# A fused convolution and SwiGLU kernel: the sixth block pair put in the Strassen form, with a new hand-written order of all engines

## The chip, the cores and the metric

The kernel runs on one core of a Trainium2 chip. The metric is the device time of one execution in microseconds (us). Five engines work side by side: TensorE (PE, matrix products; PEld is its weight load), VectorE (DVE), ScalarE (ACT), GpSimd (POOL) and SyncE (SP, which here only issues DMAs). Each engine runs its own instructions strictly in the order in which they were recorded, and waits at an instruction until the semaphores that it names have been reached.

## The reference, cut to what matters

```python
# x: (8, 4096, 192), weight: (8 heads, 7 taps)
w = softmax(weight, axis=-1)
y[b, s, h, g] = sum_k w[h, k] * x_pad[b, s + k, h, g]       # causal, 7 taps, 24 channels a head
y = y.reshape(32768, 192)
xn = y / sqrt(mean(y * y, axis=-1) + 1e-6) * rms_g
g = xn @ w_gate                                             # 192 -> 1536
v = xn @ w_val                                              # 192 -> 1536
out = (g * sigmoid(g) * v) @ w_out                          # 1536 -> 192, float32
```

## The kernel before

**Tiling.** The 32768 tokens are worked on in 32 "pairs" of 1024 tokens (two groups of 512), numbered 0 to 31. Pairs 0 and 1 take plain fp32 products while the weights are made ready; pairs 2 to 31 take the form that this text is about. The 1536 hidden columns are cut into 12 blocks of 128, and these into six block pairs j = 0 to 5. For each j and for the two token groups there are four results ("cells") a, b, c, d, each with a gate half and a value half in PSUM. The contraction over 192 rows runs in three slices of 64 rows, written as a 2x2 block scheme. Each fp32 operand is split into three fp32r parts, so one product of two blocks is three passes, each once for the gate half of the array and once for the value half: one word of LINE, such as `P6.4`, is six matmul instructions (recorded at L899).

**Two forms of a block pair.** `FORM[j]` says which. Form 0 (plain) takes 12 products, `Aa` to `Ed`. Form 1 (Strassen) takes 11, named P1 to P7 and Q1 to Q4, and pays for it with elementwise work: `f1` copies cell a into cell b's bank once P1 is in it, `f3` copies cell c into SBUF once P5 is in it, `f4` writes c = b + that copy after P6 and before P7, and `f5` writes d = b + that copy after P7 and before Q3, P4 and Q4. Before, j = 0, 2, 4 have form 1.

**After the products.** `g` (ACT) takes Silu of a cell's gate half, `m` (DVE) multiplies it with the value half into `ht` and so frees the PSUM bank pair. There are four bank pairs; each cell holds one from its first product to its `m`. The products with w_out are in a Strassen form too: 42 steps `oN.j` of eight narrow matmuls each (L923), fed by sums `h1` to `h4` of the four cells (L950). At the end X, Y, Z are brought together (`c1`, `s7`, `c2`, `C22`, `C21`, `T..`) and stored (`st`).

**The input side, for the next pairs.** `ld` loads x (8 DMAs of one head each), `cv0` to `cv6` are the convolution taps (`cv0` on ACT, the others on DVE), `sq`, `red`, `pow`, `bc`, `mul` normalise, `pl` writes the result to a scratch in DRAM (8 DMAs), `ft` reads it back transposed (6 DMAs). `x1` to `x4` make the Strassen sums of the operands, and `n`, `l`, `d` split operand group 0 to 4 into its three parts.

**What sets the order.** Everything is in three hand-written lists of words. A word is engine letter (V DVE, G POOL, A ACT, S SP), name and block; a trailing `-` means the pair before, `+` the next pair, `++` the one after that; `pN` issues the next N words of LINE on PE. FIRST is the window in which pair 1 is computed and the weights of pairs 2 to 31 are made (each `W` is one step of `prepare`); ORDER is one steady window and is run for w = 2 to 32. Within an engine the words are the order of execution. LINE is the order of PE's products and steps.

**The ring.** The split weights (`wd`, in DRAM) come through ten slots of 192 KB. When the last product that needs a slot has been issued, `ring_load` puts the load of the next piece in SP's queue at that place. `R` (`ring_start`) issues the first ten; the ring takes over the memory that held pair 2's operands, so its first load waits until pair 2's splits have read them.

```python
        n = next(taken)
        q, (j, o) = 2 + n // len(pieces_of), pieces_of[n % len(pieces_of)]
```

A plain block pair uses 6 pieces, a Strassen one 9.

Of the kernel before, what the change touches and what calls it, by code (L numbers as in the profile page):

```python
# [11 lines left out]
F32 = mybir.dt.float32  # L12
# [8 lines left out]
def kernel(  # L21
# [21 lines left out]

    T = 512
    PT = 2 * T
    NJ = PT // P
    HALO = K - 1
    HP = P // 2
# [5 lines left out]
    NU = FC // NF  # L54
    assert KP == 3 and D % HP == 0 and S % PT == 0 and FC % NF == 0
    assert NJ >= HALO
    NB = S // PT
    PAIRS = B * NB
# [9 lines left out]
    SPAN = 1509  # L68
    SPLIT = 2.0**-12
    HIGH = 0xFFFFF000  # L70
    FORM = (1, 0, 1, 0, 1, 0)
    PLAIN = tuple((j, c) for j in range(NP) for c in "abcd")
    ORDER = (
        "Vd.0 An.4 An.3 Ac2- p5- Gh4.2- Vl.2 Vd.4 Vh4.3- Vl.3 Vd.3 Vl.0 Vd.2 Vh4.0- Vh4.5-",
        "p8- Gh4.4- Gh4.1- VT11- VC22- p2- p1 Gl.4 Acv0+ Af1.0 VT22- VC21- p1- VT21- p3 Vcv1+",
        "p1 Af3.0 Ast1.2- Vcv2+ Vf4.0 p3- p3 Aga.0 Ast1.0- Vcv3+ VT12- Vma.0 Sst0.2- Agc.0",
        "Ast0.3- p1 Vf5.0 p2 Vcv4+ p1 Vmc.0 Vcv5+ p2 Sst1.3- p1 Sst0.4- Sst0.0- Agb.0 Ast1.1-",
        "Agc.1 Ast0.1- Vmb.0 p2 Vcv6+ Agd.0 p2 Aga.1 Vmd.0 Vma.1 Vmc.1 p1 Asq+ Vred+ p1 Af1.2",
        "Sst1.4- Gh1.0 Agb.1 Vmb.1 p1 Gpow+ p3 Af3.2 p1 Vf4.2 p4 Aga.2 Agd.1 Vma.2 Vbc+ Vf5.2",
        "Gmul+ p1 Agc.2 p1 Apl.0+ Apl.1+ Apl.2+ p1 Vmd.1 Vmc.2 p6 Agd.2 Agb.2 Apl.3+ Vmb.2",  # L80
        "Vmd.2 Apl.4+ p1 Agb.3 Aga.3 Apl.5+ p1 Vmb.3 Vma.3 p4 Af1.4 Vf3.4 Agc.3 Apl.6+ Apl.7+",
        "p3 Vmc.3 p1 Vf4.4 p2 Aga.4 Gh1.1 p1 Agd.3 Aft.0+ Sft.2+ Vma.4 Vf5.4 Vh3.1 Sft.3+",
        "Aft.1+ Sld.0++ Vmd.3 Sft.4+ Sld.1++ Sft.5+ Sld.2++ Sld.3++ Sld.4++ Sld.5++ Sld.6++",
        "Sld.7++ p7 Gh1.3 Agc.4 Agd.4 Vmc.4 Vmd.4 Agb.4 p1 Vh1.2 Vh3.0 Vmb.4 p7 An.0+ p1",
        "Aga.5 Agd.5 p1 Vh1.4 An.1+ Vx1+ Vmd.5 Vma.5 p1 Gh3.3 p2 Gh3.2 Agb.5 p2 Gh3.4 p2 Gx3+",
        "Agc.5 Vd.1+ p1 Vh2.0 Vmc.5 Vh2.1 Vmb.5 Vh1.5 Vh2.2 Vh3.5 Vl.1+ Vh2.5 Vh2.4 Ac1 p1",
        "Gx2+ An.2+ p6 Gh2.3 Gx4+ As7 p8",
    )
    FIRST = (
        "p1 Vcv5+ W p2 Vcv6+ p1 Aga.0 Vma.0 p2 Asq+ W W p1 Agb.0 W Vmb.0 W p1 Vred+ p2 Agc.0",  # L90
        "Vmc.0 W p1 Gpow+ W W W p1 W p1 Agd.0 W Vmd.0 p1 Vbc+ Gh1.0 p1 Gmul+ p1 Aga.1 Vh3.0 W",
        "Vma.1 p1 W W W W p1 W p1 Agb.1 Apl.0+ Vmb.1 p1 Apl.1+ p1 Apl.2+ W p1 Agc.1 Apl.3+ W",
        "W W Vmc.1 Apl.4+ p1 W W Apl.5+ p1 Apl.6+ p1 Agd.1 Apl.7+ Vmd.1 p1 Gh1.1 W p1 W W W",
        "p1 Aga.2 Vh3.1 W Vma.2 W p3 Agb.2 Vmb.2 W p1 W W W p1 W p1 Agc.2 W Vmc.2 p3 Agd.2 W",
        "Vmd.2 p1 W W W Vh1.2 W p1 W p1 Aga.3 Gh3.2 Vma.3 p2 W p1 Agb.3 W W W Vmb.3 p1 W W p1",
        "Aft.0+ p1 Aft.1+ Agc.3 Sft.2+ Vmc.3 p1 Sft.3+ W p1 Sft.4+ W W W Sft.5+ p1 Agd.3 W",
        "Vmd.3 W p1 Gh1.3 p2 Aga.4 Gh3.3 Vma.4 W p1 W W p1 W p1 Agb.4 W Vmb.4 p3 Agc.4 W",
        "Vmc.4 p1 W p2 Agd.4 An.1+ Vmd.4 p1 Vx1+ Sld.0++ Vh1.4 p1 Gx3+ Vd.1+ p1 Aga.5 Gh3.4",
        "Vma.5 Vl.1+ Sld.1++ p1 Gx2+ p1 An.2+ p1 Agb.5 Sld.2++ Gx4+ Vmb.5 p1 Sld.3++ p2 Agc.5",
        "Sld.4++ Vmc.5 p1 Sld.5++ p1 Sld.6++ Agd.5 p1 An.0+ Vmd.5 p1 Vh2.0 Sld.7++ Vh1.5 p2",  # L100
        "Gh2.3 Vh3.5 Vh2.5 p1 Vh2.1 p1 Vh2.4 p1 Ac1 Vh2.2 p2 R p7 As7 p7",
    )
    LINE = (
        "P1.0 P5.0 P6.0 P2.0 Q1.0 P7.0 P3.0 Q2.0 Ac.1 Q4.0 Q3.0 P4.0 Bc.1 Ec.1 Aa.1 Ba.1 Ea.1",
        "Ab.1 Eb.1 P1.2 Bb.1 P5.2 P6.2 P2.2 Q1.2 Ad.1 Ed.1 P7.2 P3.2 Bd.1 Q2.2 Q3.2 Q4.2 Aa.3",
        "Ba.3 P4.2 Ea.3 Ab.3 Bb.3 Eb.3 Ac.3 Bc.3 P1.4 P5.4 Ec.3 P6.4 P2.4 Q1.4 Ad.3 Bd.3 P7.4",
        "Ed.3 Q2.4 P3.4 Q4.4 P4.4 Ad.5 Q3.4 Ed.5 Aa.5 Ea.5 Ab.5 Bd.5 Ac.5 Bc.5 Ba.5 Bb.5 Ec.5",
        "Eb.5 o1.0 o1.5 o1.3 o1.1 o1.4 o1.2 o7.0 o7.3 o7.4 o2.0 o7.1 o7.2 o2.5 o6.0 o7.5 o6.2",
        "o2.3 o6.1 o2.4 o6.4 o6.3 o6.5 o4.4 o2.1 o4.1 o5.0 o2.2 o5.5 o4.3 o5.3 o4.5 o5.2 o5.4",
        "o5.1 o4.2 o4.0 o3.5 o3.2 o3.3 o3.1 o3.4 o3.0",  # L110
    )

    cst = ctx.enter_context(tc.tile_pool(name="cst", bufs=1))
# [23 lines left out]
    def load_head(p, b, t0, h, eng="S"):  # L137

        t = x_sb[p]

        def get(dst, tb, h, dims, r):
            row = x[b, t0 + tb * TB + r - HALO, h * GS :]
            src = bass.AP(
                tensor=row.tensor, offset=row.offset, ap=[dims, [D, TB + HALO - r], [1, GS]]
            )
            queue(eng).dma_start(out=dst, in_=src)  # L146

        first = int(t0 == 0)
        if first and h == 0:
            nc.gpsimd.memset(t[0:H, 0:HALO, :], 0.0)  # L150
            get(t[0:H, HALO:, :], 0, 0, [GS, H], HALO)
        get(t[first * H + h :: H], first, h, [TB * D, P // H - first], 0)

    def load_part(p, h, eng):

        if h == 0:
            x_sb[p] = xs.tile([P, TB + HALO, GS], F32, name="xh")
        load_head(p, p // NB, (p % NB) * PT, h, eng)
# [75 lines left out]
    lent = spc.tile([P, 2 * KP * T], F32, name="ring")  # L234
    early = room1[:, 10 * T + NJ * D : 10 * T + 4 * NJ * D].rearrange("p (i n) -> p i n", i=3)
    kept = [early[:, i].rearrange("p (j d) -> p j d", d=D) for i in range(3)]
# [139 lines left out]
    scr = {}  # L376
# [235 lines left out]
    def place(p):  # L612

        if p >= PAIRS:
            return
        y = yn.pop(p)
        xd = scr[p] = dram.tile([D, PT], F32, name="xd")  # L620
        to = xd[:].rearrange("(h a) (b t) -> h b a t", a=GS, t=TB)
        for first in range(2) if p == 1 else (0,):
            q = nc.scalar if first else nc.sync
            for h in range(first, H, 2 if p == 1 else 1):
                q.dma_start(out=to[h], in_=y[h::H])
            yield
# [92 lines left out]
    def blocks(o):  # L719

        kind = {2: 1, 4: 1, 6: 1, 8: 1, 9: 0}.get(o)
        mine = [j for j in range(NP) if kind in (None, FORM[j])]
        step = {b - a for a, b in zip(mine, mine[1:])}
# [304 lines left out]

    def put_away(p, h, eng):
        if h == 0:  # L1030
            scr[p] = dram.tile([D, PT], F32, name="xd")
        to = scr[p][:].rearrange("(h a) (b t) -> h b a t", a=GS, t=TB)
        queue(eng).dma_start(out=to[h], in_=yn[p][h::H])

    def ahead(eng, name, p):

        act, *at = name.split(".")
        i = int(at[0]) if at else 0
        if act[0] == "x":
            x_sum(int(act[1]), eng, p)  # L1040
        elif act in ("n", "l", "d"):
            split(act, i, eng, p)
        elif act == "ft":
            fetch(p, i, eng)
        elif act == "pl":
            put_away(p, i, eng)
        elif act == "ld":
            load_part(p, i, eng)
        elif act[0:2] == "cv":
            tap_of(p, int(act[2]), eng)  # L1050
        else:
            {"sq": square, "red": reduce, "pow": factor, "bc": spread, "mul": scale}[act](p)
# [271 lines left out]
```

## Time and profile before

| | before |
|---|---|
| median of 3 runs | 2499.0 us (2497.2 to 2500.96) |
| the profiled execution | 2498.01 us |
| its span, first to last instruction | 2496.2 us |
| mean granted TensorE clock | 0.999 |
| PE busy | 2477.4 us, 99% of the span |
| DVE / ACT / POOL busy | 2013.4 / 926.6 / 852.5 us |
| HBM read, written | 349.26 MB, 58.39 MB |

The busy time of PE counts overlapped matmuls once. From 216 us on the profile repeats itself: 30 windows, one for each of pairs 2 to 31, with an o-phase of PE (steps at L923) between two product phases (L899).

### The profile page before, as it was taken

How to read it: one execution, taken by the hardware profiler on the slowest of the kernel's cores; microseconds unless marked ns; L12 is line 12 of the kernel's file. 1: busy time of each engine (PE TensorE's matmuls, PEld its weight loads, DVE VectorE, ACT ScalarE, POOL GpSimd, SP SyncE). 2: the span in 40 equal slices, each digit the busy share in tenths (PEclk: the TensorE clock that was granted, in tenths of full speed). 3: DMA queues.
4: the chain of work that ended last, by engine and by line, in shares of the span. 5: the costliest groups of instructions: out<-in, count | busy, mean ns of one | idle time of the engine just before them, and what ended most of it. 6: DMA issues, size and time to landing. Idle time of an engine off the chain costs nothing.

```text
span 2496.2 us, 69094 instructions
## 1 busy us (share of the span) xinstructions
PE 2477.4 (99%) x29140; PEld 1932.4 (77%) x29140; DVE 2013.4 (81%) x2482; ACT 926.6 (37%) x1349; POOL 852.5 (34%) x640
## 2 busy tenths in 40 slices
PE   8999999999999999999999999999999999999999
PEld 5647778877777787777877788777777877778887
DVE  8668888788878788878888788888787888888864
ACT  6443334333333333333333343333333333333331
POOL 0553333423243324343333333233433233333331
PEclk9999999999999999999999999999999999999999
DMA  7365667766678666677666677666686666786652
GB/s 150 59 189 152 155 170 192 173 180 157 156 171 205 169 166 158 160 180 193 172 160 157 168 192 176 179 154 157 170 201 172 165 158 162 181 197 171 159 140 81
DMA packets 701735, 412.22 MB, mean 165 GB/s; under 512 B 506610, under 2 KB 687730, under 8 KB 701426
## 3 DMA queue, kind: packets, MB, share of 16 engines
q1 hardware_dynamic: 540176, 353.65, 56.1%
q10 hardware_dynamic: 161250, 54.16, 9.7%
q8 instruction: 230, 3.77, 0.6%
q14 instruction: 79, 0.65, 0.1%
HBM read 349.26 MB, written 58.39 MB: 163 GB/s over the span
## 4 chain that ended last, share of the span: by engine, by line
PE 96%; DMA 2%; SPq 1%; DVE 0%; ACT 0%; issue 0%; ACTq 0%; DVEq 0%
PE ps L899 56%; PE ps L923 34%; PE ps L871 2%; PE ps L1070 2%; DMA xb<-xd 1%; PE ps L1111 1%; SPq L146 0%; SPq L229 0%; DMA ht<-in_moe_w_gate_dram 0%; DMA x<-in_x_dram 0%; DMA ht<-in_moe_w_val_dram 0%; ACT tt L973 0%; DVE ht L980 0%; SPq L631 0%; ACT o_sb L1119 0%
## 5 line engine op out<-in xcount | busy, mean ns | idle before, releaser
L899 PE MATMUL ps<-part,ring 64*128 64x512 f32 x12420 | 1442.9, 389 | 0.0
L899 PEld LDWEIGHTS ps<-part,ring 64*128 64x128 f32 x12420 | 1185.8, 184 | 236.5 <-issue 18.0
L973 ACT ACTIVATE tt<-ps 128x512 f32<-128x512 f32 x744 | 430.9, 598 | 726.4 <-PE ps L899 586.4
L980 DVE TENSOR_TENSOR ht<-ps,tt 128x512 f32<-128x512 f32 x744 | 495.5, 684 | 190.5 <-ACT tt L973 185.3
L923 PE MATMUL ps<-ht,wo_sb 128*32 128x384 f32 (+2 forms) x6696 | 443.1, 380 | 3.3 <-DVE ht L980 3.3
L923 PE MATMUL ps<-ht,x 128*32 128x256 f32 (+2 forms) x6696 | 441.9, 379 | 0.0
L950 POOL TENSOR_TENSOR ht<-ht 128x512 f32<-128x512 f32 x186 | 283.7, 1538 | 433.3 <-PE ps L923 377.1
L950 POOL TENSOR_TENSOR hs<-ht 128x512 f32<-128x512 f32 x93 | 120.2, 1293 | 834.2 <-DVE ht L980 832.3
L923 PEld LDWEIGHTS ps<-ht,wo_sb 128*32 128x32 f32 x6696 | 296.2, 110 | 121.9 <-issue 21.5
L923 PEld LDWEIGHTS ps<-ht,x 128*32 128x32 f32 x6696 | 302.5, 110 | 90.6
L435 DVE SCALAR_TENSOR_TENSOR y<-xh,tp,y 128x1536 f32<-128x1536 f32 x186 | 342.5, 1841 | 1.3
L667 ACT COPY ps<-ps 128x384 f32<-128x384 f32 (+1 forms) x121 | 104.1, 860 | 408.7 <-PE ps L899 311.7
L967 DVE TENSOR_TENSOR ps<-ps,tt 128x1024 f32<-128x1024 f32 x180 | 221.3, 1229 | 42.1 <-PE ps L899 35.0
L667 ACT COPY tt<-ps 128x384 f32<-128x384 f32 (+1 forms) x122 | 91.0, 746 | 227.0 <-PE ps L923 207.8
L923 PE MATMUL ps<-hs,x 128*32 128x128 f32 (+2 forms) x2232 | 161.0, 379 | 0.0
L950 DVE TENSOR_TENSOR ht<-ht 128x512 f32<-128x512 f32 x186 | 126.5, 693 | 8.0 <-POOL hs L950 4.6
L923 PEld LDWEIGHTS ps<-hs,x 128*32 128x32 f32 x2232 | 108.9, 110 | 27.7
L667 ACT CAST part<-xb 128x1024 fp32r<-128x1024 f32 x87 | 91.3, 1050 | 104.0 <-DMA xb<-xd 67.1
L950 DVE TENSOR_TENSOR ht<-hs,ht 128x512 f32<-128x512 f32 x155 | 122.4, 806 | 2.9 <-PE ps L923 1.1
L950 DVE TENSOR_TENSOR hs<-ht 128x512 f32<-128x512 f32 x93 | 116.4, 1252 | 2.1
L815 DVE SCALAR_TENSOR_TENSOR part<-part,xb 128x1024 fp32r<-128x1024 f32 x87 | 105.5, 1213 | 0.0
L813 DVE TENSOR_TENSOR part<-xb,part 128x1024 fp32r<-128x1024 f32 x87 | 105.4, 1212 | 0.0
(136 smaller groups left out, 1460.1 us busy)
## 6 DMA issues: line engine op xcount, KB each, us to landing
ring<-wd SPq DMA_DIRECT2D x1350, 192.0 KB
xb<-xd SPq DMA_DIRECT2D x122, 256.0 KB
xd<-xh ACTq DMA_DIRECT2D x240, 96.0 KB
xh<-in_x_dram SPq DMA_DIRECT2D x192, 105.0 KB
xb<-xd ACTq DMA_DIRECT2D x58, 256.0 KB
out_dram<-o_sb ACTq DMA_DIRECT2D x93, 96.0 KB
wd<-part SPq DMA_DIRECT2D x5, 1152.0 KB
xh<-in_x_dram SPq DMA_DIRECT2D x56, 98.4 KB
```

The lines of the kernel that those rows point to most:

```text
L435: nc.vector.scalar_tensor_tensor(out=y, in0=xk, scalar=w, in1=y, op0=ALU.mult, op1=ALU.add)
L667: nc.scalar.copy(out=dst, in_=src)
L813: e.tensor_tensor(out=split_of(g, 1).bitcast(F32R), in0=src, in1=high, op=ALU.subtract)
L815: nc.vector.scalar_tensor_tensor(out=split_of(g, 2).bitcast(F32R), in0=high, scalar=1.0 + SPLIT, in1=src, op0=ALU.mult, op1=ALU.subtract,)
L871: nc.tensor.matmul(out=self.both(j, c)[:, h, :], lhsT=wf[HALF[h], k, 2 * j + f, :], rhs=rb[HALF[h], k, g, :], start=(k == 0), stop=(k == K ...
L899: nc.tensor.matmul(out=self.both(j, c)[:, h, :], lhsT=left[HALF[h]], rhs=right[HALF[h]], start=(first and q == 0), stop=True, skip_group_c ...
L923: nc.tensor.matmul(out=self.acc(b)[i * Q : (i + 1) * Q, at : at + n], lhsT=left, rhs=cols, start=fresh, stop=True, skip_group_check=True, ...
L950: engine[eng].tensor_tensor(out=dst, in0=a, in1=b, op=op)
L967: nc.vector.tensor_tensor(out=self.both(j, c), in0=self.both(j, "b"), in1=s5, op=ALU.add)
L973: nc.scalar.activation(out=tt[:, t, :], in_=self.both(j, c)[:, 0, :], func=AF.Silu)
L980: nc.vector.tensor_tensor(out=self.hv(j, "abcd".index(c)), in0=self.both(j, c)[:, 1, :], in1=tt[:, t, :], op=ALU.mult,)
L1070: nc.tensor.matmul(out=bank(h, bks[h])[:], lhsT=wf[HALF[h], AT[h][k], u * NF + f, :], rhs=xb[HALF[h], g, k, :], start=(k == 0), stop=(k == ...
```

## The change

- `FORM` gets a 1 for j = 5: four Strassen block pairs and two plain ones. LINE has 68 products in place of 69; with that go one more `f1`, `f3`, `f4` and `f5` in each window, and 48 ring pieces in place of 45.
- ORDER, FIRST and LINE are written anew. In ORDER the stores to the scratch (`pl`) and all reads of it (`ft`) go to SP's queue and come later; `x2`, `x4`, `c2`, `s7` and one `n` move to VectorE; one `l` and, on balance, three `h` sums move to GpSimd.
- In FIRST, six `h1` and `h3` sums go from GpSimd to VectorE, and one `h2` the other way, and all eight loads of pair 3's x come after `R`.
- `prepare` covers all six blocks for four weight sums that it made for three, and two blocks for one that it made for three.
- The scratch `xd` has rows of 1152 floats, of which 1024 are used.

```diff
+    PITCH = PT + P
-    FORM = (1, 0, 1, 0, 1, 0)
+    FORM = (1, 0, 1, 0, 1, 1)
     ORDER = (
-        "Vd.0 An.4 An.3 Ac2- p5- Gh4.2- Vl.2 Vd.4 Vh4.3- Vl.3 Vd.3 Vl.0 Vd.2 Vh4.0- Vh4.5-",
-        "p8- Gh4.4- Gh4.1- VT11- VC22- p2- p1 Gl.4 Acv0+ Af1.0 VT22- VC21- p1- VT21- p3 Vcv1+",
-        "p1 Af3.0 Ast1.2- Vcv2+ Vf4.0 p3- p3 Aga.0 Ast1.0- Vcv3+ VT12- Vma.0 Sst0.2- Agc.0",
...
-        "p3 Vmc.3 p1 Vf4.4 p2 Aga.4 Gh1.1 p1 Agd.3 Aft.0+ Sft.2+ Vma.4 Vf5.4 Vh3.1 Sft.3+",
-        "Aft.1+ Sld.0++ Vmd.3 Sft.4+ Sld.1++ Sft.5+ Sld.2++ Sld.3++ Sld.4++ Sld.5++ Sld.6++",
-        "Sld.7++ p7 Gh1.3 Agc.4 Agd.4 Vmc.4 Vmd.4 Agb.4 p1 Vh1.2 Vh3.0 Vmb.4 p7 An.0+ p1",
-        "Aga.5 Agd.5 p1 Vh1.4 An.1+ Vx1+ Vmd.5 Vma.5 p1 Gh3.3 p2 Gh3.2 Agb.5 p2 Gh3.4 p2 Gx3+",
-        "Agc.5 Vd.1+ p1 Vh2.0 Vmc.5 Vh2.1 Vmb.5 Vh1.5 Vh2.2 Vh3.5 Vl.1+ Vh2.5 Vh2.4 Ac1 p1",
-        "Gx2+ An.2+ p6 Gh2.3 Gx4+ As7 p8",
+        "p1- Vx2 Vl.0 Gh4.3- Gh4.2- Vx4 Vc2- An.1 An.2 Vl.2 p11- An.3 p2- Vd.0 p1- Vd.1",
+        "Vh4.4- Vd.3 p1 VT11- Vd.2 VC22- Gh4.0- Gx3 Gh4.5- Acv0+ Af1.0 An.4 Gh4.1- Gl.1 Vl.3",
+        "VT22- VC21- p6- VT21- Vcv1+ p2 Af3.0 VT12- p1 Gl.4 p4 Vf4.0 Vd.4 Aga.0 Agb.1 p2",
+        "Agc.0 p1 Vcv2+ Vma.0 Vmb.1 p1 Vf5.0 Vmc.0 p3 Aga.1 Agd.0 p1 Vcv3+ p2 Vma.1 Vmd.0",
+        "Agc.3 p3 Af1.2 Vcv4+ p2 Vmc.3 Agb.0 Vmb.0 p3 Vcv5+ Aga.2 Af3.2 Vf4.2 p2 Agd.3 Vma.2",
+        "Vcv6+ p3 Agc.2 p1 Vmd.3 Vf5.2 Asq+ p3 Vmc.2 Sst1.4- Sst0.1- p3 Agd.2 Agc.1 Vred+",
+        "Ast1.2- p1 Agb.2 Vmd.2 Vmc.1 Vmb.2 p1 Af1.4 p2 Gpow+ Agd.1 Af3.4 p3 Vmd.1 Vbc+ Vf4.4",
+        "Gh1.2 Gmul+ Aga.4 Vma.4 p6 Vf5.4 Spl.0+ Spl.1+ p2 Vh1.1 Gh1.0 Agb.3 Agc.4 Vmb.3",
+        "Vmc.4 p1 Agd.4 Agb.4 Sst1.1- Spl.2+ Spl.3+ p1 Vmd.4 Vmb.4 p2 Spl.4+ Spl.5+ Spl.6+",
+        "Spl.7+ Sst1.0- Sst0.3- Af1.5 p4 Aga.3 Sft.0+ Sft.1+ Sft.2+ Sft.3+ Sst0.4- Sft.4+",
+        "Vf3.5 Vf4.5 p1 Sft.5+ Sst0.2- Sld.0++ p3 Vma.3 Vf5.5 Aga.5 Agc.5 p3 Vma.5 Vh3.1 p1",
+        "Gh3.0 p1 Gh1.3 Sld.1++ Gh3.3 Sld.2++ Vh3.2 Agb.5 Agd.5 p2 Vmd.5 Vmb.5 p3 Sst0.0-",
+        "Sld.3++ Sld.4++ Sld.5++ Sld.6++ Sst1.3- Sld.7++ Gh2.0 p1 Gh1.5 Vh1.4 Vh3.4 Vh2.3",
+        "Vh2.4 Vmc.5 Vh2.1 Vh3.5 Ac1 Vh2.2 p8 Gh2.5 Vn.0+ p1 Vx1+ Vs7 p4",
     )
     FIRST = (
...
-        "Vmc.4 p1 W p2 Agd.4 An.1+ Vmd.4 p1 Vx1+ Sld.0++ Vh1.4 p1 Gx3+ Vd.1+ p1 Aga.5 Gh3.4",
-        "Vma.5 Vl.1+ Sld.1++ p1 Gx2+ p1 An.2+ p1 Agb.5 Sld.2++ Gx4+ Vmb.5 p1 Sld.3++ p2 Agc.5",
-        "Sld.4++ Vmc.5 p1 Sld.5++ p1 Sld.6++ Agd.5 p1 An.0+ Vmd.5 p1 Vh2.0 Sld.7++ Vh1.5 p2",
-        "Gh2.3 Vh3.5 Vh2.5 p1 Vh2.1 p1 Vh2.4 p1 Ac1 Vh2.2 p2 R p7 As7 p7",
+        "Vmc.4 p1 W p2 Agd.4 Vx1+ Vmd.4 p1 Vh1.4 p2 Aga.5 Vh3.4 Vma.5 p3 Agb.5 Vmb.5 p3 Agc.5",
+        "Vmc.5 p2 Agd.5 p1 Vn.0+ Vmd.5 p1 Gh2.0 Vh1.5 p2 Vh2.1 Vh3.5 Gh2.5 p1 Vh2.3 p1 Vh2.4",
+        "p1 Ac1 Vh2.2 p2 R p5 Sld.0++ p3 Vs7 p4 Sld.1++ Sld.2++ Sld.3++ Sld.4++ Sld.5++",
+        "Sld.6++ Sld.7++",
     )
     LINE = (
...
+        "P1.0 P5.0 P6.0 Q1.0 Ab.1 P2.0 Bb.1 Eb.1 Q2.0 P3.0 P7.0 Aa.1 Ea.1 Ba.1 Q4.0 Ac.3 Ec.3",
...
+        "Q4.4 Q3.4 P4.4 Aa.3 P1.5 P5.5 Ea.3 P6.5 Ba.3 Q1.5 P2.5 P7.5 P3.5 Q2.5 Q3.5 P4.5 Q4.5",
+        "o1.0 o1.5 o1.1 o1.3 o1.4 o1.2 o7.0 o7.3 o6.0 o2.3 o7.1 o2.2 o6.3 o7.4 o7.5 o7.2 o6.1",
+        "o6.4 o4.1 o2.0 o6.2 o6.5 o4.0 o2.5 o4.4 o2.1 o5.1 o5.2 o2.4 o4.5 o4.3 o5.5 o4.2 o5.3",
+        "o5.0 o5.4 o3.2 o3.5 o3.4 o3.0 o3.1 o3.3",
     )
@@ place, and the same in put_away
-        xd = scr[p] = dram.tile([D, PT], F32, name="xd")
+        xd = scr[p] = dram.tile([D, PITCH], F32, name="xd")[:, 0:PT]
```

## The prediction

> **What bounds the kernel now.** I read the page's busy shares first, then the chain of waits over one window, then the timelines where two engines meet. The share says TensorE; the chain says that it is TensorE in every window, with nothing between.
>
> ```profile
> PE 2477.4 (99%) x29140; PEld 1932.4 (77%) x29140; DVE 2013.4 (81%) x2482; ACT 926.6 (37%) x1349; POOL 852.5 (34%) x640
> ```
>
> The chain of waits of one window, in order of time (start us, us, what):
>
> ```profile
> 1276.31 0.89 PE ps L899 x6
> 1277.20 0.79 PE ps L923 x8
> 1277.98 2.94 PE ps L899 x24
> 1280.93 2.09 PE ps L923 x24
> 1283.01 44.03 PE ps L899 x384
> 1327.05 24.85 PE ps L923 x304
> 1351.90 0.90 PE ps L899 x6
> ```
>
> The window is 1351.90 - 1276.31 = 75.6 us and holds no wait. The six pieces lie on straight lines: a product (x6) costs (44.03 - 2.94) / 60 = 0.685 us, a step (x8) (24.85 - 2.09) / 35 = 0.65 us, and each change of kind costs something more: 0.89 - 0.685 = 0.20 us on entering products, 0.79 - 0.65 = 0.14 us on entering steps. There are three such pairs of changes in a window. So the path is 69 products, 42 steps and 3 x 0.34 us.
>
> The third view is a timeline of VectorE and GpSimd when both read two operands from SBUF.
>
> ```profile
> 1243.06 1.29 POOL L950 TENSOR_TENSOR ht<-ht 128x512 f32<-128x512 f32 x1
> ...
> 1243.19 1.71 DVE L950 TENSOR_TENSOR hs<-ht 128x512 f32<-128x512 f32 x1
> ...
> 1244.82 0.68 DVE L950 TENSOR_TENSOR ht<-ht 128x512 f32<-128x512 f32 x1
> ```
>
> The same sum takes VectorE 0.68 us alone and 1.71 us here: it ends 0.55 us after GpSimd's. So the two exclude each other; the page's rows of f4, m and the transposes, with at most one SBUF operand, keep their length beside GpSimd. I call two-SBUF-operand work "port work".
>
> The fourth is the start of the ring in w = 2, on SP and VectorE:
>
> ```profile
> 184.04 7.42 SPq L146 DMA_DIRECT2D xh<-in_x_dram  x8
> 209.01 8.18 SPq L785 DMA_DIRECT2D ring<-wd  x11
> ```
>
> ```profile
> 207.65 1.22 DVE L815 SCALAR_TENSOR_TENSOR part<-part,ring 128x1024 fp32r<-128x1024 f32 x1
> ```
>
> The first ring load is issued when pair 2's last split is read (207.65 + 1.22 = 208.87), 6.9 us before P1.0 at 215.88; pair 3's x is loaded well before.
>
> **Part by part, against the profiled 2498.01 us (1 us under the median of 2499.0).**
>
> One product fewer in 30 windows: 30 x 0.685 = -20.6 us. All of it is on the path.
>
> Fewer changes of kind. The new PE order has P1.0, then six o3 steps, then all the products: two pairs of changes, not three. 30 x 0.34 = -10.3 us.
>
> Late reads. In four windows TensorE waits at the first step, after VectorE's `x1` had waited for `ft` (642.9 us in the trace); the gaps are 0.59, 1.05, 0.63 and 0.98 us. `x1` now stands after the sums, behind `n`, and `ft` has some 8 us more. -3.2 us.
>
> The sixth block's elementwise work: f4 and f5 at 1.23 us, f3 on VectorE 1.23 us (as j = 4 had before), f1 1.00 us on ACT. They add no path time if they fit between the products: after P7.5 come only P3.5 and Q2.5, 1.37 us, before Q3.5 needs f5 (0.04 to start, 1.23 + 0.05): 0.05 us left. f1.5 has 0.25 us left before P6.5, f4.4 0.25 us before P7.4, f4.5 0.8 us. I take 0 for these; if `mb.4` is 0.5 us late, f1.5 costs 0.25 us a window.
>
> Moves between engines: VectorE gains f4, f5, x2, x4, `n`, c2, s7 and gives three sums and an `l`: 62.6 us of 75.6 becomes about 65 of 74.6. GpSimd goes from 26.2 to about 30 us. Neither is full; the o-phase is, for port work. From the last product to `Ab.1` (whose bank T12 frees) lie 42 steps, 4 products and the changes, 30.8 us. In it VectorE does eight `h` and three `x` (0.60 us each back to back), seven `l` and `d` (1.13), `n` (0.6) and a tap (1.73), 16.8 us; GpSimd nine of 1.23 us and an `l` of 2.3 us, 13.4 us. Sum 30.2 of 30.8 us. Followed in order, with VectorE keeping the port while its ops follow each other, and GpSimd slipping in at a PSUM op, T12 ends 30.6 us after the last product with `n` at 0.6 us, and 31.3 with `n` at 1.14. No row has this `n` on VectorE: the nearest are the copy of 128x512 in SBUF, 0.42 us (L553), and the copy of 128x1024 from PSUM, 1.225 us (L669); I take 0.6, by the first, which also stays in SBUF. So 0 to 0.8 us a window are lost here (the upper end with `ma.0` behind it late too); with margins of 0.1 us everywhere I take 0.25: 30 x 0.25 = +7.5 us (0 to 24).
>
> The Trainium skill, "VectorE: DVE Perf Modes", section "Mode 2×_2P — use both read ports for one tensor", says that an fp32 copy within SBUF uses both read ports and gives two elements a cycle; from its 0.96 GHz and some 150 cycles of start I estimate 0.69 us for `n`. By that T12 would be on time and the 7.5 us would be about 0; no run here shows this op.
>
> SP's queue: `pl` (8 issues of some 0.58 us) and two more `ft` now stand between ring loads. `pl.0` waits for `mul`; behind it wait ring pieces of j = 5. The closest ring load has 5.6 us from its place to its first use (4.2 us before); loads land 2 to 4 us after issue, and the queue gives at most 1.6 us of delay there. 0 us; if `mul` were 2 us late, about 0.5 us a window. Pair w+2's x lands some 12 us after the last product, cv0 needs it by 22. 0 us. ACT loses its DMA issues: 0, it had 48 us idle.
>
> FIRST and w = 2. TensorE's plain products (62 us) cover the larger `prepare`: 2 MB more to `wd`, its DVE and POOL ops up by about 4 us each, less six sums on POOL. +1 us (0 to 3). But pair 2's last readers of the ring's memory are now `d.2` behind T11 on VectorE, and `l.1` behind h4.3, h4.2, h4.0, x3, h4.5, h4.1 on GpSimd, each behind a step. After the last product at 191.0 us, o2.4 ends 19.0 us later; h4.4 0.6, d.3 1.13, T11 0.65, d.2 1.2: 213.7 at the earliest; `l.1`, by the port order above, 27.5 us after, 218.5. I take the later: it is the same crowded port. The ten ring loads take 5.2 us to issue (209.0 to 214.2). Behind them on SP now stand all eight loads of pair 3's x, 8.2 us (their packets ran from 186.2 to 194.4): 232 us. ACT waits for them at `cv0` (1.58 us) with f1.0 (1.00 us) behind it, which P6.0 needs: 234.7, against 191.0 + 29.4 = 220.4. +14 us once (9.5 if `d.2` decides; 15.5 at most).
>
> The rest (row pitch of the scratch, order of the last stores): 0, off the path, at the end +-1.
>
> Sum: -20.6 - 10.3 - 3.2 + 7.5 + 1 + 14 = -11.6: 2486.4, near 2487 on the scale of the median.
>
> **The rivals.**
>
> *The order holds.* No loss at the port, and `d.2` starts the ring: -34.1 + 9.5 = 2474. For it: before, an o-phase as dense (some 26.6 us of port work up to the first tap's end, which fills it) ran without a wait. Against it: the margin of T12 is 0.1 us.
>
> *The port takes it back (slower).* Place: `l.1` takes the port just before the tap `cv1`, T12 waits behind both, `Ab.1` waits for its bank, and f4.0, the taps and `ma.0` follow late. Price: T12 and `ma.0` late by 1.0 us in each window, +30: -34.1 + 14 + 1 + 30 = +11, 2509. It decides from (34.1 - 15) / 30 = 0.64 us a window. For it: 30.2 of 30.8 us taken, and 0.7 us if `n` takes 1.14. Against: VectorE has about 2 us of waits in the o-phase that could take up a slip. The Trainium skill, "SBUF — State Buffer", section "Who interferes with whom", has the same exclusion for whole instructions, whoever starts first; the 1.71 us row agrees.
>
> *Late transfers.* A ring piece or `ft` comes late in most windows, because SP holds `pl`, `ft` and `ld` in one queue: 1.5 us a window, 2525. For it: one queue in order; against: 5.6 us of room for 2 to 4 us.
>
> *The change does not save what it says.* The PE list of the changed program has 12240 products' matmuls at L899's place, not 12420, and the two-run order; this can be left out.
>
> **How the numbers follow.** Forecast 0.45, order holds 0.27, port 0.22, late transfers 0.06. A measurement here tells 0.2%, 5 us, from no change. The forecast case (2480 to 2495) and the second are faster; of the first case a little, and of the port case a quarter, lie within 5 us; the rest is slower. Faster 0.66, same 0.12, slower 0.22. The range leaves out late transfers and the far ends: 2470 to 2510.
>
> **What would show it.** Window period 74.6 us where the order holds, 74.8 in my forecast, over 75.2 in the port case, then with waits of PE on DVE o_sb (T12) before a product of `Ab.1`; four pieces of chain a window, not six; a gap of 9 to 15 us between 214 and 236 us, ended by ACT's f1.0 after the x loads; no gap at the first step. If the x loads land before 222 us, or the gap is missing, the w = 2 step is wrong; if a window has gaps elsewhere, the port step is.

## The result and the profile after

The changed kernel takes 2714.2 us (median of 4 runs, 2710.8 to 2718.7) against 2498.4 us before: a ratio of 1.0863, 95% interval 1.0843 to 1.0884. It is slower by 8.6%, where 2487 us was forecast. Its lines stand one further down than before (products L900, steps L924, `h` L951, `d` L816, `l` L814, `C22` L998). The profiled execution spans 2708.6 us, 212.4 us more than before.

First the page's busy times of the changed kernel:

```profile
PE 2537.2 (94%) x28960; PEld 1980.2 (73%) x28960; DVE 2318.0 (86%) x2577; ACT 945.0 (35%) x1317; POOL 1083.2 (40%) x697
```

PE issues 180 matmuls fewer, as the change says, and yet is busy 60 us longer. VectorE is busy 305 us longer for 95 instructions more, GpSimd 231 us longer for 57 more: 3 to 4 us for each added one, though none that was added takes much over 1.2 us on VectorE or 2.3 us on GpSimd by itself. The mean granted clock is 0.967 (before 0.999). So something makes instructions longer on three engines.

The chain of waits over one window shows where (start us, us, what):

```profile
1146.38 46.54 PE ps L900 x401
1192.92 10.56 PE ps L924 x128
...
1209.45 3.78 DMA xh<-in_x_dram
1213.24 0.02 issue
1213.26 2.30 DVE part L816
1215.56 1.31 DVE ht L951
1216.87 1.41 issue
1218.28 1.21 DVE part L816
1219.49 0.56 DVE o_sb L939 x2
1220.05 1.11 DVE part L816
1221.15 0.48 DVE tt L998
1221.63 0.14 issue
1221.77 6.35 PE ps L924 x48
```

Before, a window was PE and nothing else. Now, after 128 matmuls of the o-phase, the chain leaves PE, passes through SP's issues (left out here) and a load of x, and comes back through VectorE: `d` (L816), `h4.4` (L951), `d`, `T11` (L939), `d.2`, and last `C22` (L998), which releases the first o3 step. The waits view counts the same wait, once in each window from the second on and once, with 0.75 us, at the end (us in total, times, longest; the second line is for `s7`, a copy on VectorE, and is nearly all 1.63 us in every fourth window):

```profile
PE ps L924 <- DVE tt L998: 118.5, 30, 4.1
PE ps L924 <- DVE tt L670: 11.6, 8, 1.6
```

and the timeline of PE shows what follows it:

```profile
1216.71 0.96 PE L900 MATMUL ps<-part,ring 64*128 64x512 f32 x6
1221.77 6.35 PE L924 MATMUL ps<-ht,wo_sb 128*32 128x384 f32 x72 [4.09 <-DVE tt L998]
```

These 72 matmuls are the six o3 steps. (A step has twelve matmul records in the timeline, not eight; eight is what the chain counts of them.) They take 4.11 us at full speed (the fences of e5 and e9 show it), and 6.35 here. So each window pays twice: 4.06 us of waiting, and then a stretch in which the granted clock of the trace is 0.5, for 3.41 or 6.83 us that begin in the wait or at most 1 us behind it. The window takes 81.90 us (median of 29), not 74.6.

Why `C22` is late is in the timeline of VectorE and GpSimd ahead of it:

```profile
1209.99 4.49 POOL L951 TENSOR_TENSOR ht<-ht 128x512 f32<-128x512 f32 x2
1211.03 4.53 DVE L816 SCALAR_TENSOR_TENSOR part<-part,xb 128x1024 fp32r<-128x1024 f32 x2
1214.43 3.38 POOL L814 TENSOR_TENSOR part<-xb,part 128x1024 fp32r<-128x1024 f32 x1
1215.48 2.87 DVE L951 TENSOR_TENSOR ht<-ht 128x512 f32<-128x512 f32 x1
1218.28 1.21 DVE L816 SCALAR_TENSOR_TENSOR part<-part,tt 128x1024 fp32r<-128x1024 f32 x1
```

Read the pairs: GpSimd's two sums take 2.25 us each (1.29 alone), VectorE's two `d` 2.27 each (1.21 alone), GpSimd's `l.1` 3.38 (2.38 alone), VectorE's `h4.4` 2.87 (0.68 alone). Each engine waits out one whole instruction of the other, then does one of its own. Only at 1218.28, when GpSimd has nothing more to do there, is a `d` back to 1.21. VectorE has no idle time from 1195 to 1221.6 us. Between the last product (1192.92) and `C22`, its ops last some 10 us longer than alone: two sums +0.20 and +0.97, `n` +1.08, three `x` +1.08, +0.63 and +1.09, one `l` +0.63, two `d` +2.18, `h4.4` +2.19.

In the whole trace after 230 us there are 606 moments at which one engine ends a two-operand SBUF instruction (L951, L814, L816, L828) while the other's is waiting. In 606 of them the other engine comes next. In 371 of the 606 the engine that ended had its own next one ready at once, so that it could have gone again; only these tell of turns. In the trace of before there were only 299 such moments, and the other engine came next in 241. But only 92 of the 299 were contested, and in 58 of these the same engine went again. So turns are what the order of the changed kernel shows, and not a rule without exception.

### The profile page after: what moved, and what is told of

It reads as the page before. It is cut to its first block, busy times and chain, and to the rows that moved or that the text cites. A ratio compares the mean times of both kernels' runs of the same rounds, so it can differ in the third digit from the quotient of the medians.

```text
span 2708.6 us, 69190 instructions
## 1 busy us (share of the span) xinstructions
PE 2537.2 (94%) x28960; PEld 1980.2 (73%) x28960; DVE 2318.0 (86%) x2577; ACT 945.0 (35%) x1317; POOL 1083.2 (40%) x697
## 4 chain that ended last, share of the span: by engine, by line
PE 67%; DVE 15%; DMA 6%; SPq 5%; issue 4%; POOL 2%; ACT 1%; DVEq 0%; ACTq 0%; POOLq 0%
PE ps L900 50%; PE ps L924 16%; DVE part L816 6%; DVE ht L951 2%; DVE part L814 2%; DMA ring<-wd 2%; SPq L786 2%; SPq L147 2%; DMA xh<-in_x_dram 2%; DMA xb<-xd 1%; POOL ht L951 1%; PE ps L1112 1%; DVE tt L828 1%; DMA wd<-part 1%; DVE o_sb L939 1%
## 5 line engine op out<-in xcount | busy, mean ns | idle before, releaser
L900 PE MATMUL ps<-part,ring 64*128 64x512 f32 x12240 | 1432.2, 391 | 15.3 <-ACT ps L668 8.2
L900 PEld LDWEIGHTS ps<-part,ring 64*128 64x128 f32 x12240 | 1178.4, 184 | 254.9 <-issue 19.6
L981 DVE TENSOR_TENSOR ht<-ps,tt 128x512 f32<-128x512 f32 x744 | 491.9, 685 | 147.8 <-ACT tt L974 144.9
L924 PE MATMUL ps<-ht,wo_sb 128*32 128x384 f32 (+2 forms) x6696 | 477.7, 424 | 118.5 <-DVE tt L998 118.5
L924 PEld LDWEIGHTS ps<-ht,wo_sb 128*32 128x32 f32 x6696 | 339.3, 122 | 234.5 <-issue 167.6
L951 POOL TENSOR_TENSOR ht<-ht 128x512 f32<-128x512 f32 x215 | 382.7, 1792 | 154.6 <-DVE ht L981 114.5
L924 PE MATMUL ps<-ht,x 128*32 128x384 f32 (+2 forms) x6696 | 421.1, 380 | 17.9 <-DVE tt L670 11.6
L924 PEld LDWEIGHTS ps<-ht,x 128*32 128x32 f32 x6696 | 290.7, 110 | 114.0 <-DVE tt L670 22.1
L968 DVE TENSOR_TENSOR ps<-ps,tt 128x1024 f32<-128x1024 f32 x240 | 295.9, 1233 | 83.9 <-ACT tt L668 38.9
L668 ACT COPY ps<-ps 128x1024 f32<-128x1024 f32 (+1 forms) x151 | 134.0, 887 | 222.8 <-PE ps L924 108.8
L951 DVE TENSOR_TENSOR ht<-ht 128x512 f32<-128x512 f32 x157 | 200.8, 1295 | 5.1 <-PE ps L924 3.9
L951 POOL TENSOR_TENSOR hs<-ht 128x512 f32<-128x512 f32 x120 | 167.9, 1400 | 48.5 <-DVE ht L981 48.5
L951 POOL TENSOR_TENSOR ht<-hs,ht 128x512 f32<-128x512 f32 x62 | 92.3, 1489 | 202.5 <-DVE ht L951 102.8
L816 DVE SCALAR_TENSOR_TENSOR part<-part,xb 128x1024 fp32r<-128x1024 f32 x87 | 165.2, 1924 | 0.0
L668 ACT COPY tt<-ps 128x1024 f32<-128x1024 f32 x90 | 91.6, 1018 | 198.2 <-PE ps L900 195.6
L924 PE MATMUL ps<-hs,x 128*32 128x384 f32 (+2 forms) x2232 | 144.1, 379 | 0.0
L814 POOL TENSOR_TENSOR part<-tt,part 128x1024 fp32r<-128x1024 f32 x30 | 83.2, 2775 | 150.6 <-ACT part L668 150.6
```

The source lines that it names most:

```text
L668: nc.scalar.copy(out=dst, in_=src)
L814: e.tensor_tensor(out=split_of(g, 1).bitcast(F32R), in0=src, in1=high, op=ALU.subtract)
L816: nc.vector.scalar_tensor_tensor(out=split_of(g, 2).bitcast(F32R), in0=high, scalar=1.0 + SPLIT, in1=src, op0=ALU.mult, op1=ALU.subtract,)
L900: nc.tensor.matmul(out=self.both(j, c)[:, h, :], lhsT=left[HALF[h]], rhs=right[HALF[h]], start=(first and q == 0), stop=True, skip_group_c ...
L924: nc.tensor.matmul(out=self.acc(b)[i * Q : (i + 1) * Q, at : at + n], lhsT=left, rhs=cols, start=fresh, stop=True, skip_group_check=True, ...
L951: engine[eng].tensor_tensor(out=dst, in0=a, in1=b, op=op)
```

## The experiments

The theory after reading the trace: in this order the two engines take strict turns at the port, so each GpSimd sum that falls among VectorE's costs VectorE its whole length. That makes `C22` 4 us late, and the idle TensorE then runs slowly for a while. The rivals: transfers that come late (the chain reaches back through SP's issues to `DMA xh<-in_x_dram`); too much work on VectorE itself, whoever else uses the port; and, for the second part, another wait that only looks like slow matmuls.

**C22 one place earlier (e1).** Only `C22` moves ahead of `d.2`, which it doesn't need.

```diff
-  "Vh4.4- Vd.3 p1 VT11- Vd.2 VC22- Gh4.0- ...
+  "Vh4.4- Vd.3 p1 VT11- VC22- Vd.2 Gh4.0- ...
```

> One word moved: C22 is done by VectorE ahead of d.2, no longer behind it. Theory A (turns at the port): C22 is late because every two-operand SBUF operation of VectorE ahead of it waits out one of GpSimd's; taking one of them (d.2, 1.09 us of port) from in front of it moves C22 some 1.1 us forward, and the gap before the first o3 step shrinks from 4.05 to about 2.9 us. If the half-speed matmuls behind the gap stay, 30 x 1.1 = 33 us: about 2680 us; if they go with the shorter gap, another 30 x 2.6 us: about 2605 us. Theory B (late transfers: the chain of waits runs through the x and ring loads): the gap stays 4 us, 2714 us.

Measured: 2659.6 us, ratio 1.0629 (1.0612 to 1.0647), between the two times expected. The wait falls from 4.06 to 2.93 us, by exactly the 1.13 us of one `d`. The slow stretch now comes only in part of the windows: in 19 of the 28 windows with a wait of 2.9 us the 72 matmuls take 5.35 to 6.84 us until the next product starts, in 9 they take 4.04, and windows of that kind are as short as 78.3 us. (In one more window the wait was 1.89 us, and they took 4.04.) So the wait is VectorE's list ahead of `C22`, and after 2.9 us of idling TensorE is slow in some windows and not in others.

**Without five GpSimd sums (e2).** `h4.0`, `h4.1`, `h4.2`, `h4.3` and `h4.5` are left out; the steps that use them read cells that were not summed. VectorE's list is unchanged.

```diff
-  "p1- Vx2 Vl.0 Gh4.3- Gh4.2- Vx4 Vc2- An.1 ...
-  "Vh4.4- Vd.3 p1 VT11- Vd.2 VC22- Gh4.0- Gx3 Gh4.5- Acv0+ Af1.0 An.4 Gh4.1- Gl.1 Vl.3",
+  "p1- Vx2 Vl.0 Vx4 Vc2- An.1 ...
+  "Vh4.4- Vd.3 p1 VT11- Vd.2 VC22- Gx3 Acv0+ Af1.0 An.4 Gl.1 Vl.3",
```

> Work left out: the five h4 sums that GpSimd does in the o-phase (blocks 0, 1, 2, 3, 5) in every window, so five o3 steps use unsummed cells. Nothing else moves. Theory A: five turns of 1.14 us at the port fall away in front of C22, 5.7 us against a gap of 4.05: no gap before the o3 steps, no half-speed matmuls, window 75.5 to 77 us, 2520 to 2570 us. Theory B: x, ft and ring loads are issued and land as before, so the gap stays at 3 us or more: 2690 us or more.

Measured: 2535.5 us, ratio 1.0137 (1.0122 to 1.0152). The wait for `C22` is gone but for 0.7 us at the end of the run, the clock is 0.996, and most windows take 75.3 to 76.7 us (every fourth 77.3 to 78.2). VectorE's timeline, in the same place as above:

```profile
1144.24 2.35 DVE L816 SCALAR_TENSOR_TENSOR part<-part,xb 128x1024 fp32r<-128x1024 f32 x2
1146.51 0.68 DVE L951 TENSOR_TENSOR ht<-ht 128x512 f32<-128x512 f32 x1
```

The two `d` that took 4.53 us take 2.35, and `h4.4` takes 0.68 instead of 2.87. VectorE does the same instructions as in the changed kernel, so its own amount of work is not what makes `C22` late. (The kernel is still slower than before: its w = 2 window takes 91.1 us, the first long run of products begins 5 us later, and the other windows, 76.0 us in the median, are not shorter as a whole than before's 75.6.)

**Without the x loads (e3).** From pair 4 on the loads of x are left out, and with them the memset of the buffer's head on GpSimd; the taps read what lies there.

```diff
+        if p > 3:
+            x_sb[p] = kept_x[0]
+            return
```

> Work left out: from pair 4 on the eight x loads are not made (nor the small memset on GpSimd that goes with them in every fourth pair); the taps read what the tile holds. SP's queue is 5 us shorter in every window and cv0 waits for no load. Theory A: the usual window stays 81.9 us with its gap of 4.05 us; only the fourth windows (83 to 85 us) come down to 81.9: 2690 to 2712 us. Theory B: with the loads the wait goes, windows of 75 to 76 us, 2510 us.

Measured: 2702.9 us, ratio 1.0803 (1.0782 to 1.0825). The waits view of this kernel (its lines are four further down again):

```profile
PE ps L928 <- DVE tt L1002: 117.9, 30, 4.1
```

The wait is the same without the loads that the chain named, and in e2, where all loads stay, it is gone. The late-transfers theory falls for all but 11 us of the loss. About as much sits in every fourth window, which took 83 to 85 us and now takes 81.9 to 82.1. There, in the changed kernel, GpSimd clears the head of a new x buffer (the memset, L151), and this instruction waits for a transfer, up to 13.1 us, with the `h` sums behind it. This run leaves out the loads and the memset at once, so it doesn't tell which of the two the 11 us belong to; the memset is the reading of the trace.

**x of pair 3 ahead of the ring (e4).** In FIRST the eight loads of pair 3's x go before `R`, as in the kernel before.

```diff
-  "Vmc.4 p1 W p2 Agd.4 Vx1+ Vmd.4 p1 Vh1.4 p2 Aga.5 Vh3.4 Vma.5 p3 ...
+  "Vmc.4 p1 W p2 Agd.4 Vx1+ Vmd.4 Sld.0++ ... Sld.3++ p1 Vh1.4 p2 Aga.5 Vh3.4 Vma.5 Sld.4++ ... Sld.7++ p3 ...
...
-  "p1 Ac1 Vh2.2 p2 R p5 Sld.0++ p3 Vs7 p4 Sld.1++ Sld.2++ ...
+  "p1 Ac1 Vh2.2 p2 R p8 Vs7 p4",
```

> In FIRST the eight loads of pair 3's x are put ahead of the start of the ring, where the kernel before had them. The step of w = 2 as predicted: the gap of 8.16 us before P6.0 goes (the other, 5.94 us before P1.0, waits for the ring and stays), with it what follows at half speed: 8 to 11 us less, 2703 to 2706 us. Rival: cv0 is late for another reason too, and the gap stays: 2714 us.

Measured: 2707.5 us, ratio 1.082 (1.0804 to 1.0836), 6.7 us less than the changed kernel. Two gaps open the changed kernel's window of w = 2:

```profile
224.49 1.65 PE L900 MATMUL ps<-part,ring 64*128 64x512 f32 x6 [5.94 <-DMA ring<-wd]
...
240.99 4.63 PE L900 MATMUL ps<-part,ring 64*128 64x512 f32 x20 [8.16 <-ACT ps L668]
```

With the loads ahead the second gap (8.16 us) is gone, the first stays at 6.2, and the window takes 84.5 us instead of 95.1. Not all of those 10.6 us are left in the whole: the first long run of products begins 0.6 us later, and in the profiled execution two of the fourth windows take 85 us that took 83.

**C22 ahead of everything that it doesn't need (e5).** `C22` goes before `h4.4`, `d.3`, `T11` and `d.2`.

```diff
-  "... Vd.0 p1- Vd.1",
-  "Vh4.4- Vd.3 p1 VT11- Vd.2 VC22- Gh4.0- ...
+  "... Vd.0 p1- Vd.1 VC22-",
+  "Vh4.4- Vd.3 p1 VT11- Vd.2 Gh4.0- ...
```

> One word moved further than in the first run: C22 ahead of h4.4, d.3, T11 and d.2, so that it is the first thing VectorE does after d.1. Theory A: C22 needs only the last o5 step; it ends about when P1.0 does, the gap of 4.05 us before o3 is gone and with it all half-speed matmuls (2.6 us). The crowd behind it is not gone: what was pushed back is late next, 1.4 us before P5.0 (bank of Z, freed by C21) and 1.1 us before Ab.1 (bank of X, freed by T12, the place the prediction named). Window 81.9 - 4.05 - 2.6 + 2.5 = 77.8 to 78.3 us, 2590 to 2610 us. If the crowd were the order alone and not the port, nothing would be late next: 75 us, 2510 us.

Measured: 2618.3 us, ratio 1.0471 (1.0456 to 1.0487), 8 us above the range expected; the clock is back at 0.996, the o3 steps run without a wait, the window takes 78.36 us. PE's timeline behind the o3 steps:

```profile
1186.48 4.11 PE L924 MATMUL ps<-ht,wo_sb 128*32 128x384 f32 x72
1192.24 2.34 PE L900 MATMUL ps<-part,ring 64*128 64x512 f32 x18 [1.65 <-issue]
1195.66 4.62 PE L900 MATMUL ps<-part,ring 64*128 64x512 f32 x38 [1.08 <-DVE o_sb L939]
```

The delay has moved on: 1.65 us before P5.0 (the view names no releaser; VectorE's next L998 instruction, `C21`, ended 0.10 us before) and 1.08 us before `Ab.1`, which waits for T12. This last is the place, and nearly the price, of my rival "the port takes it back". It appears only once the wait ahead of it is out of the way. Moving a word cannot repair it: the list up to T12 is too long as a whole.

**GpSimd off the port (e6).** The five `h4` sums, `x3` and `l.1` go from GpSimd to VectorE, at their places.

```diff
-  "p1- Vx2 Vl.0 Gh4.3- Gh4.2- Vx4 ...
-  "Vh4.4- Vd.3 p1 VT11- Vd.2 VC22- Gh4.0- Gx3 Gh4.5- Acv0+ Af1.0 An.4 Gh4.1- Gl.1 Vl.3",
+  "p1- Vx2 Vl.0 Vh4.3- Vh4.2- Vx4 ...
+  "Vh4.4- Vd.3 p1 VT11- Vd.2 VC22- Vh4.0- Vx3 Vh4.5- Acv0+ Af1.0 An.4 Vh4.1- Vl.1 Vl.3",
```

> Nothing left out: the seven two-operand operations that GpSimd does in the o-phase ahead of C22 and C21 (h4 of blocks 3, 2, 0, 5, 1, x3, l.1) are done by VectorE, at the same places of the order. Theory A: on VectorE they hold the port for 0.54 (h, x) and 1.08 us (l) where GpSimd held it 1.14 and 2.25; VectorE's stretch gets shorter although it does more: 6 x 0.60 + 1.17 = 4.8 us less port time in all, of which what now stands ahead of C22 decides. Gap of 4.05 gone or below 1.5 us, no half-speed matmuls, new waits of 2 to 3 us behind it at P5.0: window about 80 us, 2640 to 2670 us, faster than 2714 by more than 1.5%. If VectorE's load and not the port bounds the stretch (86% busy already), the seven operations (5 us) make it longer: window 84 us or more, 2780 us.

Measured: 2633.3 us, ratio 1.0533 (1.0514 to 1.0551), 7 us below the range expected; clock 0.991. The page:

```profile
PE 2494.6 (95%) x28960; PEld 1940.4 (74%) x28960; DVE 2264.0 (86%) x2792; ACT 941.7 (36%) x1317; POOL 644.2 (25%) x482
```

VectorE has seven instructions more in each window, and yet the kernel is 81 us faster than the changed one and VectorE is busy less (2264 us, not 2318). The first wait at o3 is 0.79 us (now for a sum of VectorE); behind the o3 steps come 2.63 us, or 0.45 and 1.04. In this stretch the two engines together got the port work done later than VectorE does alone. But VectorE alone is too full for this order as well.

**TensorE kept busy through the wait (e9).** Sixteen matmuls on old operands, whose result nobody reads, stand between P1.0 and the first o3 step. Nothing else changes; `C22` comes no earlier.

```diff
-  "Vh4.4- Vd.3 p1 VT11- ...
+  "Vh4.4- Vd.3 p1 Twarm- VT11- ...
```

> Added work, same output: 16 products of old operands into the unused half of Z's bank, issued between P1.0 and the first o3 step of each window, where TensorE now idles for 4.05 us. VectorE's, GpSimd's and SP's lists are unchanged, so C22 comes no earlier. Theory A (the wait for C22 costs 4.05 us, and the idle TensorE then runs the next matmuls at half speed for 2.6 us more): the wait before the first o3 step stays in sum (products of no use, about 3.6 us, and a rest of 0.5 to 2 us), but the 72 matmuls behind it take 4.0 to 4.2 us instead of 6.4, the window 79.2 to 79.5 us instead of 81.9, the time 2636 to 2645 us, the mean granted clock of the profile 0.99 or more. Rival B (the 2.6 us are a second wait, for o_sb or a bank, that only looks like slow matmuls): the 72 still take 6.4 us, the window stays at 81.9, the time within 3 us of 2714, or later by what the added products cost.

Measured: 2651.5 us, ratio 1.0606 (1.0587 to 1.0625), 63 us less than the changed kernel for more work. PE's timeline (L962 is the added work):

```profile
1278.27 3.93 PE L962 MATMUL ps<-part 128*128 128x512 f32 x16
1282.39 4.11 PE L924 MATMUL ps<-ht,wo_sb 128*32 128x384 f32 x72 [0.20 <-DVE tt L1005]
```

The first o3 step still begins 4.1 us after P1.0, but the 72 matmuls take 4.04 us until the next product starts, in all 30 windows. The window falls from 81.90 to 79.53 us. That is the price of the slow stretch alone, 2.4 us in the median window (63 us in the whole, 2.2 a window), and no second wait is hidden in it. My expectation was some 6 us too low: in the 12 windows in which the stretch had been shorter, 1.3 to 1.7 us were all that there was to save.

**A new order of the same work (e7).** LINE stays as it is. In ORDER VectorE gets `x3` and all `l`, GpSimd has `h4.0`, `h4.1`, `h4.3`, `h4.4` and `h4.5`, but after most of VectorE's `x`, `l` and `d`; ACT takes back `n.0`, `c2` and `s7`; `C22` stands behind three short words only (`C21`, `T21`, `T11`). In FIRST most of pair 2's `x`, `n`, `l` and `d` come earlier, between its `W`s and `m`s, and pair 3's x comes before `R`. The memset goes to the place of `cv0`.

```diff
-        "p1- Vx2 Vl.0 Gh4.3- Gh4.2- Vx4 Vc2- An.1 An.2 Vl.2 p11- An.3 p2- Vd.0 p1- Vd.1",
-        "Vh4.4- Vd.3 p1 VT11- Vd.2 VC22- Gh4.0- Gx3 Gh4.5- Acv0+ Af1.0 An.4 Gh4.1- Gl.1 Vl.3",
-        "VT22- VC21- p6- VT21- Vcv1+ p2 Af3.0 VT12- p1 Gl.4 p4 Vf4.0 Vd.4 Aga.0 Agb.1 p2",
...
+        "Vx3 Vx2 Vl.0 Vd.0 p3- An.3 p2- Vd.3 Vx4 An.1 An.2 Ac2- p1- Vd.2 Vl.2 Vl.1 An.4 p4-",
+        "Gh4.3- p2- Vl.4 p1- Vh4.2- p2- Gh4.4- Gh4.5- Gh4.1- p1 VC21- VT21- VT11- VC22- Gh4.0-",
+        "VT22- Af1.0 p2- Acv0+ p3- Vl.3 Vd.4 Vd.1 p1- p1 VT12- Af3.0 p4 Vcv1+ p2 Vf4.0 Vcv2+",
...
```

> The same sixth Strassen block, LINE unchanged, ORDER written anew with strict turns at the port (each GpSimd operation ahead of C22 costs VectorE its whole hold) and at most eight DMAs of a queue under way; in FIRST pair 2's sums and splits are made before the last plain products and pair 3's x is loaded ahead of the ring; the memset of every fourth pair stands at cv0's place. Theory A: no wait in the steady window: 68 x 0.685 + 42 x 0.65 + 2 x 0.34 = 74.6 us, and no gap at w = 2: 2498 - 30 x 1.0 = 2468, with the startup as before, up to 2480. Theory B: transfers still come late: above 2510 us.

Measured: 2489.1 us (2487.8 to 2489.9), ratio 0.9955 (0.994 to 0.997): faster than both kernels, though not down in the 2468 to 2480 us expected. The busy times of the page, and the chain of waits over one window, which is PE alone again:

```profile
PE 2462.3 (99%) x28960; PEld 1915.9 (77%) x28960; DVE 2075.3 (83%) x2575; ACT 997.7 (40%) x1408; POOL 741.6 (30%) x608
```

```profile
1201.13 4.04 PE ps L927 x48
1205.17 46.54 PE ps L903 x396
1251.71 23.54 PE ps L927 x288
1275.25 0.89 PE ps L903 x5
```

The window is 75.00 us. Only 121 times does an engine end while the other waits at the port, not 606. VectorE has taken over `x3` and two `l` from GpSimd in each window, has two instructions fewer in all, and is yet busy 243 us less than in the changed kernel: what VectorE waited for the port had counted as busy. So the sixth Strassen pair can be had; it was the order that lost it. The gain that is left, 0.45%, is not the 1.4% that my sum gives without the port and w = 2 terms.

**A second new order (e8).** As e7, with another ORDER, in which the loads and stores lie elsewhere in SP's queue too (diff against e7).

```diff
-        "Vx3 Vx2 Vl.0 Vd.0 p3- An.3 ...
+        "Gx3 Vx2 Vh4.2- Vx4 Vl.0 An.2 p4- An.3 Vd.2 ...
...
-        "Sft.3+ Sft.2+ p1 Aga.5 Vma.3 Vf5.5 Sft.4+ Sft.5+ Sst0.0- p2 Sld.0++ Sst1.1- Sld.5++",
+        "Gh3.0 Sft.4+ Sft.0+ Sft.1+ Sft.2+ Aga.3 Vf4.5 p1 Sft.5+ Sst0.2- Aga.5 Vma.3 Vh1.2",
...
```

> Another such ORDER, with other work on GpSimd; the rest as in the reordered kernel a. Theory A: 74.6 us a window again, 2468 to 2480 us; the two differ only in how much delay they stand.

Measured: 2501.7 us, ratio 1.0009 (1.0 to 1.0019), no different from the kernel before, and over 20 us above the range expected. Its windows take 75.03 to 76.85 us. TensorE waits 0.26 to 1.72 us for a ring load (issued by SP at L789) in 13 windows, 9.0 us in all, and 0.4 to 0.7 us for VectorE in five. With the crowd at the port gone, late transfers become visible: 0.3 us a window where I had forecast 0, a fifth of the 1.5 of that rival.

## Why the prediction was wrong, point by point

**The port step failed, in its rule, its place and its price.** The rule was "VectorE keeping the port while its ops follow each other, and GpSimd slipping in at a PSUM op". The changed kernel shows turns, in 371 of 371 contested moments. The place that bears the rule out is real, but it is one place of the trace of before. There, in each window, VectorE did its `l` and `d` while GpSimd had no work, and at the end of that stretch two VectorE sums passed a waiting GpSimd sum (timeline of before):

```profile
1269.25 4.95 POOL L950 TENSOR_TENSOR ht<-ht 128x512 f32<-128x512 f32 x3 [12.51 <-PE ps L923]
```

The 12.51 us of idle time in this row are what I should have read: the kernel before keeps GpSimd off the port while VectorE does eight `l` and `d`, and the change puts GpSimd's sums there. The three sums of this row take 4.95 us, 1.1 us more than alone. All 58 exceptions to the turns stand at this place (one after a `d`, one after the first sum, in 29 windows). Why GpSimd's first instruction after its long idle time is passed over is not settled: in e6 a GpSimd `l` that comes after 17.6 us of idle time gets its turn at once, 16 times of 16. The prediction's own second row (1.71 us for a sum, "it ends 0.55 us after GpSimd's") already showed VectorE waiting out GpSimd.

The place was the wrong one because I made one sum, to `Ab.1`: 30.2 of 30.8 us. The same list has an earlier deadline. The new PE order has all o3 steps behind P1.0, and their bank needs `C22`, 24.8 us after the last product (1192.92 to 1217.68 us). VectorE got to the end of `C22` after 28.7 us. The prediction listed "no gap at the first step" as a sign, but did not work out that deadline. The rival "the port takes it back" had the right mechanism and the wrong deadline; its own place shows in e5, at 1.08 us.

The price was not 0.25 us, nor 0.8 at most: 4.06 us of waiting (e1, e2) and 2.4 us of slow matmuls (e9). No term of the sum had the second. The Trainium skill, "TensorE: Matmul & The Clock Gate", section "What's actually happening", says that TensorE's clock is halved after an idle window of some 3.4 us that runs freely, and needs about as long a busy one to come back. The traces agree on the window: their granted clock changes in steps of 3.41 us, and behind the waits for `C22` it is 0.5 for 3.41 or 6.83 us. They don't agree that TensorE must be idle for so long: after 4.06 us of idling all 29 windows are slow, after 2.9 us 19 of 28 (e1), and after 2.63 us 8 of 16 (e6). After the 1.63 us waits of e9 none is (72 matmuls in 3.9 us).

**What `n` costs.** I took 0.6 us with an upper end of 1.14. Alone, in w = 2, it takes 0.694 us, as the prediction's estimate from the Trainium skill, "VectorE: DVE Perf Modes", section "Mode 2×_2P — use both read ports for one tensor", had it. In the windows it takes 1.77: it takes its turn at the port too. That `T12` "would be on time" by that price did not hold: in e5 `Ab.1` waits 1.08 us for it.

**One product fewer, and fewer changes of kind.** Both are there: 12240 matmuls at the products' line, two runs of products and two of steps. Kernel e7 measures them without waits: 75.61 to 75.00 us, 0.6 us a window instead of 1.03. The difference is all in the long run of products. It has 67 products in 46.53 us (46.58 in the changed kernel); 44.04 us for 64, and three more at 0.685, would be 46.1. The rest of the window, steps, P1.0 and changes, takes 28.47 us, and by the prediction's prices 31.57 - 4 x 0.685 - 0.34 = 28.49. So the term for the changes of kind was right, and the products' was too large by 0.4 us a window, 13 us in all. What makes them 0.694 us instead of 0.688 was not tried, but the trace of e7 shows where more than half of it sits. From start to start most products take 0.680 us; Q2.5 and Q3.5, near the end of the run, take 0.813 and 0.802, and Q3.5 is released by `f5.5` (L971) in 29 of 30 windows. There the prediction left 0.05 us and put the cost at 0; it is some 0.25 us a window.

**Late reads.** The four waits for `x1` are gone, as said. In their place the memset at L151 holds up GpSimd in every fourth window, a step of GpSimd's list that I did not look at: 11 us, if e3's gain is all its own. In e7, where it stands elsewhere, those waits are gone.

**w = 2.** This step was right in cause and in its sum: gaps of 5.94 us (the ring's start) and 8.16 us (`f1.0` on ACT behind the x loads), 14.1 us together, +14 forecast; the loads' queue is the cause of the second by e4. The sign was not met as it was written: it named one gap of 9 to 15 us, over by 236 us, and there are two, of which the second ends at 240.99. The plain products end 4 us later than forecast (195.0 us, not 191.0), and `f1.0` 6.2 us later (240.9, not 234.7). Slow matmuls come on top.

**FIRST.** +1 us was forecast; four waits of TensorE for `m` (L981) in the plain products, of which before had none, make 3.5 us, just over the upper bound of 3.

**Late transfers.** 0 us was right for the changed kernel apart from the memset (e3) and two waits of TensorE for the ring, 0.9 us together. The chain of the changed kernel runs through SP and the x loads all the same: it has no entry for a wait at the port, and goes back from VectorE's long `d` to a transfer that e3 takes away without any effect on the wait.

**The account.** 212.4 us of span: the start of the first long run of products comes 9.3 us later, the 29 windows from there take 199.4 us more, the end 3.7. A window of 81.90 is 75.0 (e7) + 4.06 + 2.4 and some 0.4 us of smaller waits, about what e2's windows show.

## What to carry to other kernels

Where two engines share a port, do not add up busy times against a span: write down the order in which their instructions will alternate, and follow VectorE to every deadline on its list, the earliest first. An engine that the old schedule leaves idle beside another may be idle for a reason; see what the other does in that stretch before giving it work. And price a new wait of TensorE with what follows it: one of 4 us cost 6.5.

## What the runs showed of the hardware

- Turns at the port, where both engines had an instruction ready: 371 of 371 in the changed kernel, 342 of 342 in e5, 126 of 126 in e6, but 9 of 12 in e7 and 34 of 92 before. An instruction that waits costs its engine the rest of the other's whole instruction: a 0.68 us sum took up to 2.87 us.
- An idle TensorE comes back slow: the first 72 matmuls behind a 4.06 us gap took 5.3 to 6.7 us instead of 4.04. After 2.63 us of idling it happened in 8 of 16 windows (e6), after 2.9 us in 19 of 28 (e1). Sixteen useless matmuls in the gap made the whole kernel 63 us faster.
- Moving seven instructions from GpSimd onto the busier VectorE (e6) lowered VectorE's busy time by 54 us.
